# Joint first-layer tiles and a second split of four products in an attention and mixture-of-experts kernel

## The chip, the cores and the metric

The kernel is one program on one core of one Trainium2 chip. The metric is the device time of one execution in microseconds (us), from inputs in HBM to the output in HBM. Engines: PE (TensorE, matrix products), DVE (VectorE), ACT (ScalarE), POOL (GpSimd) and SP (SyncE, which here only issues DMAs). PEld is the loading of PE's weights.

## The reference

Attention in chunks of 32 queries with a little context and 8 memory keys gives `x` of 3072 tokens by 512 features. Then a mixture of 8 experts is computed densely: the routing weights `P` come from softmax logits by 8 rounds of row and column scaling, and every token goes through every expert.

```python
for e in range(E):                       # E = 8
    h = np.maximum(x @ w1[e], 0.0)       # 512 -> F = 1024
    ye = h @ w2[e]                       # 1024 -> 512
    out += P[:, e:e + 1] * ye
```

## The kernel before, in words

**Number form.** Every fp32 operand is held as two fp16 tiles, a high and a low part. One fp32 product is then three fp16 products (`PASSES`).

**Seven products.** From expert 1 on both layers are computed in a two-by-two block split with seven products P1 to P7 in place of eight. Its outputs are sums: in the first layer `c11` comes from P1 and P2; `c12`, `c22` and `c21` add P6, P7, P5, P3 and P4 in PSUM and in DVE or POOL adds. A block of weights or of tokens that a product needs is a sum of blocks made ahead (`wblock`, `xblock`).

**Units.** A unit n = 0..47 is one expert e = n // 6 on 512 tokens (u runs 0 to 5, and back for odd experts). It has two parts of work: the first layer of unit n, and the second layer (output) of unit n-1. The first layer goes over four feature groups `fp` of 256 features, two groups of 128 in each of the split's halves; here fp 0 and 1 are the front pair, fp 2 and 3 the second pair. The output of a unit is made by two generators (`output`, TH = 2), with seven products each of 12 matmuls of 128x256 in PSUM tiles yx, yy, yz. That is 168 matmuls for the output of a unit, and 168 for its first layer when no product is split again.

**A second split.** For units 15 to 47 (in unit 47 only pair 0), `inner(specs, op)` (L2389) splits three of the seven first-layer products (`op` 1, 5, 3, i.e. P2, P5, P3) by the same scheme once more: seven steps of matmuls with 128 columns. One call works for two entries at a time, the second pair of unit n and the front pair of unit n+1, so a step is six matmuls (L2447) into PSUM tiles ix, iy, iz; ACT reads them (L2498), and DVE adds (L2509, L2482), into fp32 buffers `m`, `m5`, `m3`. Where three products of both pairs are split, a unit has 126 matmuls of 128 columns in place of 72 of 256.

**First layer of one group.** `hidden` (L2552) runs the products of one fp into px, py, pz (matmuls in `product`, L2371), tiles of 128x256. Behind its matmuls each fp has: ACT reads (L2582, L2665, L2765), DVE adds (L2697, L2601, L2641), POOL adds for `c11` (L2675) and `c12` (L2717), then on the finished sums `c`: DVE sums `ss` (L2788, four of 128x256, or fewer and wider), ACT high part (L2800, 128x768) and DVE low part (L2838), ACT high part of the sums (L2830, 128x1024) and DVE low part of the sums (L2857, 128x1024). What they give, `h`, is the weight operand of the output matmuls.

**Output of a unit.** Each generator has ACT reads of its PSUM with the routing weight (L2976) and DVE adds into `acc` (L3018); POOL issues the DMAs that store `acc` (L3133), and SP issues the loads.

**Order.** A planner records tasks with a cost, a due time and dependencies. On PE each task depends on the one before (`last_pe`), so PE's order is that in which the generators are stepped; `WOVEN` (L3512) writes it out per unit, one letter per step: F, G (front pair), B, C (second pair), x, y (output), i, j, k (second split of P2, P5, P3). DVE, ACT, POOL and SP are put in order by due times, worked out from when PE uses what they make. So on those engines a row runs when it stands first in its queue and its inputs are there.

**Buffers.** Rings of tiles in SBUF: a taker waits for the last users of the tile before. Blocks of tokens come in by SP's DMAs in 256 KB pieces (`blocks`, L3463), in a ring of 10 and 11 slots.

## Time and profile before

| what | us |
|---|---|
| time, median of 3 runs | 1882.04 (1881.41 to 1883.43) |
| span of the profiled execution, first to last instruction | 1878.8 |
| PE busy in it | 1865.7 |
| DVE busy | 1511.8 |
| ACT busy | 1123.9 |
| POOL busy | 811.2 |

The span is what the engines' records cover; the time holds what lies around it as well. An engine's busy time is a sum over its instructions. A PE matmul's duration in the timeline includes the time that it drains; the rate of a run of matmuls is read from the starts of one group and the next.

### The profile page before, as it was taken

The page shows a single profiled execution, that of the slowest core. Times are in us where ns is not written, and L with a number is a line of the kernel's source. Part 1 is how long each engine was busy: PE and PEld are TensorE (multiplying, and loading weights), DVE is VectorE, ACT ScalarE, POOL GpSimd, SP SyncE. Part 2 cuts the span into 40 slices and gives each one's busy share as a digit, 9 for nine tenths or more (in the row PEclk, how much of TensorE's full clock was granted, in tenths as well). Part 3 has the DMA queues.
Part 4 walks back from the last instruction along what each step waited for, and adds up shares of the span by engine and source line. Part 5 has one row for each costly group of instructions (what it writes and reads, how often), then busy time and mean ns, then how long its engine had stood idle before and what let it go on. Part 6 is the DMA issues. An engine that isn't in the chain of part 4 may idle for free.

```text
span 1878.8 us, 52243 instructions
## 1 busy us (share of the span) xinstructions
PE 1865.7 (99%) x21167; PEld 1619.8 (86%) x21167; DVE 1511.8 (80%) x2664; ACT 1123.9 (60%) x2272; POOL 811.2 (43%) x994
## 2 busy tenths in 40 slices
PE   8999999999999999999999999999999999999999
PEld 5776676788888999999998999999999999999998
DVE  5886779788899778887889788897889778896564
ACT  6665454666676556656656665665666565565453
POOL 3631222525565345434556345643555335651231
PEclk9999999999999999999999999999999999999999
DMA  9968843297799767797677957887677976885553
GB/s 217 228 146 204 213 140 135 80 286 207 198 268 295 198 167 206 219 265 179 186 222 224 262 149 192 245 262 180 178 221 223 255 190 175 223 249 148 121 125 90
DMA packets 347293, 374.31 MB, mean 199 GB/s; under 512 B 123500, under 2 KB 261484, under 8 KB 345452
## 3 DMA queue, kind: packets, MB, share of 16 engines
q1 hardware_dynamic: 323436, 327.98, 57.1%
q0 software_dynamic: 23616, 43.00, 15.4%
q8 instruction: 166, 2.72, 0.6%
q14 instruction: 75, 0.61, 0.1%
HBM read 242.96 MB, written 133.18 MB: 200 GB/s over the span
## 4 chain that ended last, share of the span: by engine, by line
PE 96%; DVE 1%; DMA 1%; issue 1%; ACT 1%; POOL 0%; SPq 0%; POOLq 0%
PE px L2371 25%; PE yx L2371 23%; PE yz L2371 12%; PE ix_1c L2447 7%; PE yy L2371 6%; PE yp L3267 5%; PE pz L2371 4%; PE iz_1c L2447 3%; PE py L2371 2%; PE iy_1c L2447 2%; PE yp L3330 1%; PE pp L3184 1%; PE xp L1793 1%; PE sp L1715 1%; PE ta L1782 1%
## 5 line engine op out<-in xcount | busy, mean ns | idle before, releaser
L2371 PEld LDWEIGHTS <-h 128*128 128x128 f16 x6972 | 667.6, 98 | 72.9 <-DVE h L2857 0.9
L2371 PEld LDWEIGHTS <-w_all 128*128 128x128 f16 x5640 | 542.1, 98 | 64.2 <-issue 1.8
L2371 PE MATMUL yx<-w_all,h 128*128 128x256 f16 x3840 | 482.9, 273 | 0.6 <-DVE h L2857 0.6
L2371 PE MATMUL px<-x_whole,w_all 128*128 128x256 f16 x2976 | 363.0, 273 | 0.6 <-DMA x_whole<-xkeep 0.4
L3133 POOL DMA_DIRECT2D akeep<-acc x164 | 145.2, 908 | 258.9 <-DVE acc L3018 239.2
L2371 PE MATMUL yz<-w_all,h 128*128 128x256 f16 x1920 | 230.9, 273 | 0.0
L2857 DVE TENSOR_TENSOR h<-ss,h 128x1024 f16<-128x1024 f32 x158 | 198.4, 1257 | 13.5 <-ACT h L2830 13.2
L2830 ACT CAST h<-ss 128x1024 f16<-128x1024 f32 x166 | 172.6, 1040 | 51.8 <-DVE ss L2788 51.5
L2838 DVE SCALAR_TENSOR_TENSOR h<-c,h 128x768 f16<-128x768 f32 x166 | 179.2, 1084 | 9.7 <-ACT h L2800 9.7
L2788 DVE SCALAR_TENSOR_TENSOR ss<-c,ss 128x256 f32<-128x256 f32 x336 | 173.0, 515 | 3.8
L2447 PEld LDWEIGHTS <-wi 128*128 128x128 f16 x2340 | 157.0, 98 | 6.4
L2371 PE MATMUL px<-x,w_all 128*128 128x256 f16 x1248 | 152.9, 273 | 0.0
L2800 ACT ACTIVATE h<-c 128x768 f16<-128x768 f32 x166 | 137.6, 838 | 25.1 <-DVE c L2601 15.6
L962 POOL TENSOR_TENSOR w2f<-w2f 128x256 f32<-128x256 f32 x96 | 103.3, 1076 | 113.7 <-DVE wp L773 100.9
L2788 DVE SCALAR_TENSOR_TENSOR ss<-c,h 128x256 f32<-128x256 f32 (+1 forms) x248 | 145.9, 590 | 6.4 <-ACT h L2776 3.0
L3083 ACT ACTIVATE acc<-yx,pscale 128x256 f32<-128x256 f32 x82 | 38.7, 472 | 159.1 <-PE yx L2371 158.8
L962 POOL TENSOR_TENSOR w1b<-w1b 128x256 f32<-128x256 f32 x96 | 88.0, 917 | 86.6 <-ACT m_1c L2498 49.7
L2447 PEld LDWEIGHTS <-w_all 128*128 128x128 f16 x1755 | 119.5, 98 | 6.3 <-issue 0.5
L2717 POOL TENSOR_TENSOR c<-h,x_whole 128x256 f32<-128x256 f32 x130 | 101.5, 802 | 37.9 <-ACT h L2582 32.4
L2371 PE MATMUL yy<-w_all,h 128*128 128x256 f16 x960 | 114.0, 273 | 0.0
L3267 PE MATMUL yp<-w_all,h 128*128 128x512 f16 x480 | 110.3, 379 | 0.0
L2976 ACT ACTIVATE acc<-yx,pscale 128x256 f32<-128x256 f32 x164 | 76.8, 473 | 39.3 <-PE yx L2371 39.2
(287 smaller groups left out, 3077.7 us busy)
## 6 DMA issues: line engine op xcount, KB each, us to landing
x_whole<-xkeep SPq DMA_DIRECT2D x186, 256.0 KB
akeep<-acc POOLq DMA_DIRECT2D x164, 256.0 KB, 5.5
wkeep<-wp SPq DMA_DIRECT2D x48, 512.0 KB
w_all<-wkeep SPq DMA_DIRECT2D x84, 256.0 KB
w_all<-wkeep SPq DMA_DIRECT2D x42, 512.0 KB
wkeep<-wp SPq DMA_DIRECT2D x48, 384.0 KB
w2f<-in_moe_w_dram SPq DMA_DIRECT2D x32, 512.0 KB
w1fm<-in_moe_w_dram SPq DMA_DIRECT2D x28, 512.0 KB
```

The source lines that it names most:

```text
L962: lambda d=d, p=p, q=q, op=op: nc.gpsimd.tensor_tensor(d(), p(), q(), op=op),
L2371: nc.tensor.matmul(dst.t, a, b, start=(not more and n == 0), stop=(n == end), skip_group_check=more,)
L2447: nc.tensor.matmul(dst.t[:, k], left(k, op[0], wl), right(k, op[1], xl), start=(not more and n == 0 and k == 0), stop=(n == 2), skip_group ...
L2717: lambda: nc.gpsimd.tensor_tensor(c.t[:, 1], rr(1), m35[1](), op=ALU.add),
L2788: lambda: nc.vector.scalar_tensor_tensor(dst(), src(), 0.0, other(), op0=ALU.max, op1=op),
L2800: lambda: nc.scalar.activation(h.t[:, 0, 0:3], c.t, AF.Relu),
L2830: lambda: nc.scalar.copy(h.t[:, 0, 3:7], ss.t),
L2838: lambda: nc.vector.scalar_tensor_tensor(h.t[:, 1, 0:3].rearrange("p a n -> p (a n)"), c.t.rearrange("p a n -> p (a n)"), 0.0, h.t[:, 0, 0 ...
L2857: lambda: spare.tensor_tensor(h.t[:, 1, 3:7], ss.t, h.t[:, 0, 3:7], op=ALU.subtract),
L2976: lambda: nc.scalar.activation(acc.t[:, cols], src.t, AF.Copy, scale=f),
L3133: lambda a=a, dst=dst: nc.gpsimd.dma_start(dst, a.t, accum_op=ALU.add),
L3267: nc.tensor.matmul(py.t, hf.t[:, hl, where[fh], o : o + P], room(fp, WIDE * wl + DM * fh, WIDE * wl + DM * (fh + 1)), start=(fp == 0 and i ...
```

## The change

**Joint tiles.** `paired` takes the place of `hidden` for experts 1 to 7; `hidden` stays for expert 0. It works on both fps of a pair at once: px holds 128x2x256, a step is 12 matmuls (L2607) into it, and each DVE add (L2647), ACT read (L2637) and DVE sum (L2740) is 128x512 wide instead of two or more of 128x256. High and low parts (L2761, L2779, L2770, L2797) stay one for each fp, and of the sums' low parts the first of each pair is on POOL. The sums `c` have a ring of two buffers, `s` has one.

**Second split.** It begins at unit 14 (`DEEP`) for both pairs of the same unit. Expert 2 splits P2, P5, P3, as before; experts 3 to 7 split P4 as well. One call `inner(e, u, pair)` runs the three or four products of a pair together: seven steps of 9 or 12 matmuls with 128 columns (L2511), ACT reads (L2545) and DVE adds (L2556) of 128x3x128 or 128x4x128. Its results are in one buffer `m` for each pair (pair 0 in `stage_high`, pair 1 in `x_whole`), and part 3 of it is `rest`, on which the first layer works until its sums `d` and `a` (L2740) are made.

**First layer in a split unit.** P1 gives c11 (DVE, into `c`), which P6 waits for; P6 gives c12, which P7 waits for; P7 gives c22 and, with four split, c21. One POOL add of 128x512 (`m35`) joins P3's and P5's parts. The small POOL adds of `c11` and `c12` and the ACT reads between are gone.

**Order and buffers.** In `WOVEN` all fourteen steps of the second split (i pair 0, j pair 1) stand at the head of a unit. Token blocks have two rings, six slots for products 0, 4, 5 and four for 1, 2, 3, 6; the split sums of the tokens (`load_xi`) and of the weights (`fetch_wi`) come as 256 KB loads; tiles of SBUF are assigned anew.

```diff
-    def inner(specs, op=1):
-
-        nm = "_".join(str(i) for i in specs[0]) + f"c{op}"
-        (wop, xop), wsums, xsums, results = {
-            1: (P2, wi, xi, inners),
-            3: (P3, wi3, xi3, thirds),
-            5: (P5, wi5, xi5, fifths),
-        }[op]
+    inners = {}
+    ASIDES = ((0, 0), (1, 0))
+
+    def inner(e, u, pair):
+
+        nm = f"{e}_{u}_{pair}i"
+        ops = split_of(e)
+        z = len(ops)
         parts = []
         made = []
         used = []
-        for e, u, pair in specs:
+    inners = {}
+    ASIDES = ((0, 0), (1, 0))
+
+    def inner(e, u, pair):
+
+        nm = f"{e}_{u}_{pair}i"
+        ops = split_of(e)
+        z = len(ops)
         parts = []
         made = []
         used = []
-        for e, u, pair in specs:
+        for op in ops:
+            wop, xop = {1: P2, 5: P5, 3: P3, 4: P4}[op]
             tiles = [wblock(e, 2 * pair + i, 1, wop) for i in range(2)]
-            win, xin = wsums[e, pair], xsums[u]
+            win, xin = wi[e, pair, op], xi[u, op]
             x, part, xmade = xblock(u, xop)
-            parts.append((tiles, win, part, xin))
+            parts.append((tiles, win[0], part, xin[0], (0, 1, 2, 3) if op in (1, 4) else (3, 0, 2, 1)))
...
-        if op == 5:
-            m = rings["m5"].take(
-                lambda _: stage.tile([P, 2, 2, 2, P], F32, tag="stage_2", name=f"m5_{nm}")
-            )
-        elif op == 3:
-            m = rings["m3"].take(
-                lambda _: spare(5, 7).bitcast(F32).rearrange("p (k f q n) -> p k f q n", k=2, f=2, q=2)
-            )
-        else:
-            m = rings["m"].take(
-                lambda k: spare(3, 5).bitcast(F32).rearrange("p (k f q n) -> p k f q n", k=2, f=2, q=2)
-                if k
-                else stage.tile([P, 2, 2, 2, P], F32, tag="stage_3", name=f"m_{nm}")
-            )
-        z = len(specs)
-        if op == 3:
-            m5, _, ready5 = fifths[specs[0][0], specs[0][1], 2 * specs[0][2]]
-
-        which_op = op
+        m = rings["m"].take(
+            lambda k: (spare(3, 7).bitcast(F32) if k else high).rearrange(
+                "p (o f q n) -> p o f q n", o=4, f=2, q=2
+            ),
+            pair,
+        )
...
-                lambda: nc.scalar.activation(at(*to), src.t[:, 0:z], AF.Copy, scale=DOWN),
+                0.6,
...
+        inners[e, u, pair] = (m, [m11, m12, m22, read(ix, (1, 0), t4, ix)])
...
-    def hidden(e, u, fp, hs, use_at, aside, place="h"):
+    def paired(e, u, which, hs, place="h"):
+
+        nm = f"{e}_{u}_{which}"
+        fps = 2 * which, 2 * which + 1
+        px = bank("main", [P, 2, GT], f"px_{nm}")
+        c = rings["cd"].take(
+            lambda k: shaped(joint["c"] if k else both_sums(), [P, 2, 3, GT])
...
+                for f in range(2):
+                    for n, (kt, (wl, xl)) in enumerate(
+                        (kt, p) for kt in range(2) for p in PASSES
+                    ):
+                        nc.tensor.matmul(
+                            dst.t[:, f],
...
+        if (e, u, which) in inners:
+            m, made = inners[e, u, which]
+            part = lambda i: lambda: m.t[:, i].rearrange("p f q n -> p f (q n)")
+            m35 = add(
+                "POOL",
+                1.5,
+                lambda: nc.gpsimd.tensor_tensor(part(2)(), part(2)(), part(1)(), op=ALU.add),
+                made,
+                now[0],
+                [m],
+            )
+            t1 = run(px, P1, False, [], px)
+            c11 = plus(px, at(2), part(0), [t1, *made], [c, m])
+            yield
+            t6 = run(px, P6, True, [c11])
+            c12 = plus(px, at(1), part(2), [t6, m35], [c, m])
+            yield
+            rest = part(3)
+            t7 = run(px, P7, True, [c12])
+            if len(split_of(e)) == 4:
+                c22 = plus(px, at(0), part(1), [t7, *made], [c, m], px)
+                c21 = plus(px, rest, rest, [t7, *made], [m], px)
+                yield
...
+        s = rings["sd"].take(lambda k: shaped(joint["ss"], [P, 2, 4, GT]))
...
+        d = rsum(0, 0, rest, ALU.subtract, [r, c22], [m])
+        a = rsum(2, 2, rest, ALU.add, [r, c11], [m])
+        b = rsum(1, 0, lambda: s.t[:, :, 2], ALU.subtract, [a, c22])
+        g = rsum(3, 1, lambda: s.t[:, :, 1], ALU.add, [b, c12])
+        yield
...
+            aside = (which, f) in ASIDES
+            slo = add(
+                "POOL" if aside else "DVE",
+                2.15 if aside else 1.24,
...
-        "fine": "FGZiiFGiFiiGyixiyFGxyxjxjyjyjxjxjyjkkxykxykxykBkCkBCBCB",
...
+        "thirds": "ijijijijijijijFxyFxytFxyFFxyFxyBxyBtxyBxyBBxyxy",
+        "deep": "ijijijijijijijFxyFxyFxyFFxyBxyBxyBxyBxyxy",
+        "end": "ijijijijijijijFxByFxByFxByFFWBBxyxyxyxyxyxy",
...
-        specs = [(*units[n + i], 1 - i) for i in range(2) if thirded(n + i)] if not end else []
-        deep = [inner(specs, op) for op in (1, 5, 3)] if specs else []
+        inside = [inner(e, u, p) for p in range(2)] if deep else [None] * 2
```

**PE at the head of unit 25 (expert 4, second unit), before.** px is the first layer, yx the output, ix and iz the second split; "..." leaves out the rest of each group of six or twelve, and the weight loads.

```order
L2371 MATMUL px_0_3_16303<-x_whole_10012,w_all 128x256
...
L2447 MATMUL ix_1_1c_16402<-x_whole_10012,w_all 128x128
...
L2447 MATMUL iz_1_1c_16410<-xi_1_1_14807,wi_1_15351 128x128
...
L2371 MATMUL px_1_0_16374<-x_whole_9735,w_all 128x256
...
L2371 MATMUL px_1_1_16382<-x_whole_9735,w_all 128x256
...
L2447 MATMUL ix_1_1c_16402<-xi_1_1_14807,wi_1_15351 128x128
...
L2371 MATMUL px_1_0_16374<-x_whole_9735,w_all 128x256
...
L2447 MATMUL iz_1_1c_16410<-x_whole_10012,wi_1_15351 128x128
...
L2447 MATMUL ix_1_1c_16402<-xi_1_1_14807,wi_1_15351 128x128
...
L2371 MATMUL px_1_1_16382<-x_whole_9735,w_all 128x256
...
L2371 MATMUL yx_0_1_16482<-w_all,h_0_0_15813 128x256
```

The same place now; the names ending in 0i and 1i are the second split of pair 0 and of pair 1.

```order
L2448 MATMUL yz_0_1_15276<-w_all,h_late 128x256
...
L2511 MATMUL ix_1_0i<-x_whole_9177,w_all 128x128
...
L2511 MATMUL ix_1_1i<-x_whole_9177,w_all 128x128
...
L2511 MATMUL iz_1_0i<-wx_late 128x128
...
L2511 MATMUL iz_1_1i<-wx_late,p_all 128x128
...
L2511 MATMUL ix_1_0i<-wx_late 128x128
...
L2511 MATMUL ix_1_1i<-wx_late,p_all 128x128
...
L2511 MATMUL ix_1_1i<-wx_late,w_all 128x128
...
L2607 MATMUL px_1_0_15610<-x_whole_9477,w_all 128x256
...
L2448 MATMUL yx_0_0_15626<-w_all,h_all 128x256
...
L2448 MATMUL yx_0_1_15637<-w_all,h_all 128x256
```

Steps of six matmuls stood among steps of the first layer and the output. Now fourteen steps of twelve stand in one piece, and the first layer comes behind them.

**DVE at the same place, before.** acc is the output's sum, h_0_0 and h_0_1 take the low parts of sums, ss are the sums, x_whole the buffer of the second split.

```order
L2857 TENSOR_TENSOR h_0_0_15813<-ss_0_0_16068,h_0_0_15813 128x1024
L2788 SCALAR_TENSOR_TENSOR ss_0_1_16260<-c_0_1_15910,h_0_1_15816 128x2x256
L773 SCALAR_TENSOR_TENSOR wp_4_3_4_16245<-w2f_3_15992,sw,wp_4_3_4_16245 128x4x256
L3018 SCALAR_TENSOR_TENSOR acc_3_15990<-yz_0_1_16120,pscale,acc_3_15990 128x256
L2509 SCALAR_TENSOR_TENSOR x_whole_10012<-ix_0_1c_16147,x_whole_10012 128x2x128
L2788 SCALAR_TENSOR_TENSOR ss_0_1_16260<-c_0_1_15910,ss_0_1_16260 128x256 x2
L2509 SCALAR_TENSOR_TENSOR x_whole_10012<-iy_0_1c_16294,x_whole_10012 128x2x128
```

Now. ss_all from c_all and x_whole, twice, are `d` and `a` of unit 24's second pair, which read `rest` in pair 1's buffer.

```order
L3071 SCALAR_TENSOR_TENSOR acc_2_15132<-yz_0_0_15257,pscale,acc_2_15132 128x256
L3071 SCALAR_TENSOR_TENSOR acc_3_15147<-yz_0_1_15276,pscale,acc_3_15147 128x256
L2797 TENSOR_TENSOR h_all<-ss_all,h_all 128x1024
L2740 SCALAR_TENSOR_TENSOR ss_all<-c_all,x_whole_9477 128x2x256 x2
L2779 SCALAR_TENSOR_TENSOR h_all<-cs_late,h_all 128x768
L2779 SCALAR_TENSOR_TENSOR h_all<-c_all,h_all 128x768 x2
L2556 SCALAR_TENSOR_TENSOR stage_high<-iz_1_0i,stage_high 128x4x128
L2556 SCALAR_TENSOR_TENSOR stage_high<-ix_1_0i,stage_high 128x4x128
```

ACT in the same stretch, now; the row into x_whole is the first read of pair 1's second split in unit 25.

```order
L2770 CAST h_all<-ss_all 128x1024
L3139 ACTIVATE acc_0_15289<-yx_0_0_15082,pscale 128x256
L2770 CAST h_all<-ss_all 128x1024
L3139 ACTIVATE acc_1_15305<-yx_0_1_15093,pscale 128x256
L2761 ACTIVATE h_all<-c_all 128x768 x2
L2545 ACTIVATE stage_high<-ix_1_0i 128x4x128
L2545 ACTIVATE stage_high<-iz_1_0i 128x4x128
L2545 ACTIVATE x_whole_9477<-ix_1_1i 128x4x128
L2545 ACTIVATE x_whole_9477<-iz_1_1i 128x4x128
```

On DVE the low part of the sums stands between the last acc and the two sums that read pair 1's buffer, and ACT's first read into that buffer can run when both are made. Before, the reads of the second split go to buffers that take turns.

**DVE in unit 12 (first of expert 2), now.** c_all from py is the first layer's c11 of pair 1; h_late from ss_all is the low part of sums that the output of unit 11 uses.

```order
L3071 SCALAR_TENSOR_TENSOR acc_2_8635<-yy_0_0_8637,pscale,acc_2_8635 128x256
L3071 SCALAR_TENSOR_TENSOR acc_3_8655<-yy_0_1_8657,pscale,acc_3_8655 128x256
L2647 SCALAR_TENSOR_TENSOR c_all<-py_0_1_8710,c_all 128x2x256
L2797 TENSOR_TENSOR h_late<-ss_all,h_late 128x1024
L2182 TENSOR_TENSOR wx_late<-x_0_7565 128x512
L849 SCALAR_TENSOR_TENSOR wp_2_3_3_8731<-stage_high,sw,wp_2_3_3_8731 128x2x256
L886 TENSOR_REDUCE mxs<-w1fm_1_8701 128x1
```

Before, at the same place, c from px are adds of 128x256 of unit 12, and h_0_2 and h_0_3 the low parts for unit 11's output.

```order
L2601 SCALAR_TENSOR_TENSOR c_0_0_8950<-px_0_0_8899,q_2_0_0_8990 128x256
L2601 SCALAR_TENSOR_TENSOR c_0_1_8960<-px_0_1_8909,q_2_0_1_8993 128x256
L2857 TENSOR_TENSOR h_0_2_8786<-ss_0_2_8917,h_0_2_8786 128x1024
L2601 SCALAR_TENSOR_TENSOR c_0_0_8950<-pz_0_0_8964,h_0_0_8926 128x256
L2601 SCALAR_TENSOR_TENSOR c_0_1_8960<-pz_0_1_8972,h_0_1_8937 128x256
L2857 TENSOR_TENSOR h_0_3_8796<-ss_0_3_8979,h_0_3_8796 128x1024
```

The low part stood between two pairs of adds; now it stands behind one add of both groups, whose input is the PSUM tile py.

## Rows read from the trace of the kernel before

**Rows 1.** The page: the span, and busy time of each engine with its instructions.
```profile
span 1878.8 us, 52243 instructions
PE 1865.7 (99%) x21167; PEld 1619.8 (86%) x21167; DVE 1511.8 (80%) x2664; ACT 1123.9 (60%) x2272; POOL 811.2 (43%) x994
```

**Rows 2.** The page: shares of the chain that ended last, by engine.
```profile
PE 96%; DVE 1%; DMA 1%; issue 1%; ACT 1%; POOL 0%; SPq 0%; POOLq 0%
```

**Rows 3.** What PE waited for from 600 us on: total us, times, longest.
```profile
PE yx L2371 <- DVE h L2857: 0.6, 1, 0.6
PE px L2371 <- DMA x_whole<-xkeep: 0.4, 1, 0.4
PE px L2371 <- DVE c L2697: 0.2, 1, 0.2
```

**Rows 4.** PE's timeline near 1001 us: start, duration, instruction, count.
```profile
1000.84 0.50 PE L2447 MATMUL iz_1c<-x_whole,wi 128*128 128x128 f16 x6
1001.17 0.50 PE L2447 MATMUL ix_1c<-xi,wi 128*128 128x128 f16 x6
1001.51 0.82 PE L2371 MATMUL px<-x_apart,w_all 128*128 128x256 f16 x6
```

**Rows 5.** PE's timeline, 692 to 695 us.
```profile
692.13 1.47 PE L2371 MATMUL yz<-w_all,h 128*128 128x256 f16 x12
693.44 0.50 PE L2447 MATMUL ix_1c<-more,w_all 128*128 128x128 f16 x6
693.78 0.50 PE L2447 MATMUL ix_1c<-x_whole,w_all 128*128 128x128 f16 x6
694.11 0.33 PE L2447 MATMUL iz_1c<-xi,wi 128*128 128x128 f16 x3
694.28 0.33 PE L2447 MATMUL iz_1c<-more,wi 128*128 128x128 f16 x3
694.45 2.79 PE L2371 MATMUL yx<-w_all,h 128*128 128x256 f16 x24
```

**Rows 6.** The page: weight loads of the inner products, mean ns behind busy us.
```profile
L2447 PEld LDWEIGHTS <-wi 128*128 128x128 f16 x2340 | 157.0, 98 | 6.4
```

**Rows 7.** ACT's timeline, same stretch; idle time and its releaser in brackets.
```profile
692.00 0.47 ACT L2976 ACTIVATE acc<-yz,pscale 128x256 f32<-128x256 f32 x1
692.37 0.89 ACT L764 ACTIVATE ws_halves<-w1b,sw 128x256 f16<-128x256 f32 x2
693.64 0.47 ACT L2976 ACTIVATE acc<-yz,pscale 128x256 f32<-128x256 f32 x1 [0.38 <-PE yz L2371]
```

**Rows 8.** DVE's timeline, 691 to 697 us.
```profile
691.31 1.22 DVE L2857 TENSOR_TENSOR h<-ss,h 128x1024 f16<-128x1024 f32 x1
692.44 0.42 DVE L2509 SCALAR_TENSOR_TENSOR m_1c<-iy_1c,m_1c 128x256 f32<-128x256 f32 x1
696.36 0.68 DVE L2788 SCALAR_TENSOR_TENSOR ss<-c,h 128x512 f32<-128x512 f32 x1
```

**Rows 9.** DVE instructions by line and shape: busy us, mean ns, idle before.
```profile
L2857 DVE TENSOR_TENSOR h<-ss,h 128x1024 f16<-128x1024 f32 x158 | 198.4, 1257 | 13.5 <-ACT h L2830 13.2
L2788 DVE SCALAR_TENSOR_TENSOR ss<-c,h 128x512 f32<-128x512 f32 x84 | 64.1, 763 | 3.4 <-ACT h L2776 3.0
L3018 DVE SCALAR_TENSOR_TENSOR acc<-yz,pscale,acc 128x256 f32<-128x256 f32 x82 | 39.1, 478 | 17.2 <-PE yz L2371 17.0
L773 DVE SCALAR_TENSOR_TENSOR wp<-w2f,sw,wp 128x1024 f16<-128x1024 f32 x24 | 31.3, 1304 | 2.1 <-ACT wp L764 2.1
```

**Rows 10.** ACT instructions by line and shape.
```profile
L2830 ACT CAST h<-ss 128x1024 f16<-128x1024 f32 x166 | 172.6, 1040 | 51.8 <-DVE ss L2788 51.5
L2800 ACT ACTIVATE h<-c 128x768 f16<-128x768 f32 x166 | 137.6, 838 | 25.1 <-DVE c L2601 15.6 <-DVE c L2697 9.6
L1802 ACT COPY at<-ta 128x512 f32<-128x512 f32 x24 | 14.1, 587 | 7.8 <-PE ta L1782 7.7
```

**Rows 11.** What DVE waited for from 600 us on, by line.
```profile
DVE c L2697 <- PE px L2371: 54.9, 85, 1.5
```

More of the change, by code (lines that the diff above doesn't have):

```diff
@@ L56 @@
 LONG = 0.6
+BRIEF = 0.75
 LENGTHY = 0.4
@@ L61 @@
 PACED = 1
+EARLIER = 20.0
 BESIDES = 0.8
 class Task:
-    __slots__ = ("eng", "cost", "fn", "prio", "left", "ready", "end", "then", "takes", "frees", "n", "dma", "start", "size", "port", "also", "first", "lead")
+    __slots__ = ("eng", "cost", "fn", "prio", "left", "ready", "end", "then", "takes", "frees", "n", "dma", "start", "size", "port", "also", "first", "lead", "tag")
     def engines(self):
@@ L598, in sums_buf @@
     def sums_buf(kind, shape, name):
[L600 to L604 removed]
+        return rings[kind].take(lambda k: shaped(home(kind, k), shape))
     def bank(group, shape, name):
@@ L2361, in tile_chunked_attn_sinkhorn_moe, with product @@
     last_pe = [None]
-    def product(dst, pairs, more, deps, bufs=(), takes=None, parts=1, part=0):
+    def product(dst, pairs, more, deps, bufs=(), takes=None, parts=1, part=0, tag=None):
         def go():
@@ L2691, in hidden @@
[L2691 to L2705 removed]
+        py = psum("py")
@@ L2706, in hidden @@
+        q1, r1 = read(px, "q1", t1)
+        yield
+        t2 = run(py, P2, False, [], py)
+        c11 = plus(2, py, q1, [t2, r1])
+        yield
+        t6 = run(px, P6, True, [r1])
+        q6, r6 = read(px, "q6", t6)
+        yield
+        t5 = run(pz, P5, False, [], pz)
+        q5, r5 = read(pz, "q5", t5)
+        yield
+        t7 = run(px, P7, True, [r6])
+        c22 = plus(0, px, q5, [t7, r5], last=False)
         yield
-        if m is None:
-            t3 = run(pz, P3, True, [r5])
-            c12 = plus(1, pz, q6, [t3, r6])
-            yield
+        t3 = run(pz, P3, True, [r5])
@@ L2802, in hidden @@
+            lambda: nc.scalar.activation(h.t[:, 0, 0:4], c.t, AF.Relu),
+            [c11, c22, c12, c21],
             at - 6.0,
@@ L2952, in run @@
                 part,
+                "plain" if a < 3 else "sums",
             )
@@ L3111, in output @@
+        if DEEP - 1 <= n < len(units) - 1:
+            c21 = fourth()
+            yield
+            c12 = third()
+        else:
+            c12 = third()
+            yield
+            c21 = fourth()
         ended.setdefault(e, []).extend([c11, c12, c22, c21])
@@ L3552, in weave @@
         run(*front)
-        if end:
-            free = [t for g in range(6) for t in rings["wb"].last[1, 0, g].users]
-            for g in range(6):
-                rings["wb"].last[1, 0, g].closed = True
-            for i in range(2):
-                rings["w1"].after(i, free)
-            rings["w1"].n = 0
-            run(*pair(1, "w1"))
-        run(*deep[0:2])
-        run(*deep[2:3])
         run(*back)
         hidden_of.pop(n - 1)
-        behind[:] = then
-        if kind == "opening" or n == FINE * NU + 3:
-            run(*behind)
+        run(*then)
         if first_of:
@@ new lines, in weave @@
+            rings["xid"].after(2, wide)
+            fetch_wi(e, 0, begin(n))
+        if (n + 1) % NU:
+            blocks(n + 1)
+            load_xi(e, units[n + 1][1], begin(n), range(len(split_of(e))))
+        elif n + 1 < len(units):
+            if e == FINE:
+                for kind, k in (("xid", 3), ("wid", (0, 3))):
+                    rings[kind].after(k, rings["xt"].last[0].users)
+                rings["wid"].after((1, 3), [t for k in range(2) for t in rings["xg"].last[k].users])
+                load_xi(e, units[n + 1][1], begin(n), (3,))
+            for side in range(2):
+                fetch_w(e + 1, 1, side)
+                fetch_wi(e + 1, side, begin(n))
@@ L3772, in tile_chunked_attn_sinkhorn_moe @@
             expert_scale(e + 1, begin(n + 1))
+    ring("ss", range(2))
+    for i in range(2):
+        rings["ss"].after(i, rings["sd"].last[0].users)
+    rings["sd"].last[0].closed = True
     outputs(len(units) - 1, hidden_of.pop(len(units) - 1))
```

1082 lines of the change are left out of this document (513 added, 569 removed), and 12 rows, old and new, of the table TOKENS.

## The prediction, made before the run

> **What bounds the kernel now.** I read the page's busy times first: PE is busy 1865.7 of a span of 1878.8 us, the other engines 80% or less [rows 1]. Then the chain that ended last: 96% of it is PE, no other engine has more than 1% [rows 2]. Then PE's own waits from 600 us on, where every unit with a second split lies: three, 1.2 us in all [rows 3]. So PE's order runs almost without a gap, and its length is what the change can move, in two ways: the matmuls that PE has to run, and new places where PE finds its operand not made. DVE, ACT and POOL count only at such places.
>
> **The matmuls.** Twelve matmuls of 128x128 take from 1000.84 to 1001.51, 0.67 us or 55.8 ns each [rows 4]. Twelve of 128x256 start at 692.13 and the next group at 693.44: 1.31 us, 109.2 ns each [rows 5]. A split product has 126 or 168 narrow matmuls in a unit where it had 72 or 96 wide ones (three or four products). Before, 32.5 units of three: 4095 narrow in place of 2340 wide. Now four units of three and thirty of four: 4 x 126 + 30 x 168 = 5544 in place of 4 x 72 + 30 x 96 = 3168. The change therefore removes 828 wide and adds 1449 narrow: -828 x 0.1092 + 1449 x 0.0558 = -90.4 + 80.9 = **-9.5 us**. The output's matmuls, expert 0, expert 1's counts and the attention stay. The saving holds while the narrow ones keep their pace in runs of 168. The longest run that the trace has is 18, from 693.44 to 694.45, 56.1 ns each [rows 5]; at that figure the sum is -9.1.
>
> The Trainium skill, "TensorE: Matmul & The Clock Gate", section "Back-to-back issue gap", speaks against this: a sustained stream of weight load and matmul costs about 81 ns at 128 columns there, not 56. By its figure the sum would be 1449 x 0.081 - 90.4 = +27 us, an estimate. The run of 18 does not bear it out; runs of 168 are not in this trace.
>
> **DVE, ACT, POOL, DMA.** Most of their edits I cost at nothing, since PE's work hides them: the joint adds and sums need half as many instructions of twice the width (a sum of 128x512 takes 0.68 undisturbed [rows 8] and 0.76 in the mean, an add of 128x256 0.48 [rows 9]), so no engine gets more to do and DVE stays below PE. POOL, busy 43% [rows 1], loses small adds and gets `m35` and half the sums' low parts. If a queue's order is wrong this cover is gone; that is the next part. SP's loads grow by about 256 KB a unit, with wider windows of time between buffer free and use; I take 0, with 0 to +1.
>
> **New waits.** I looked for places where the rows that stand on an engine between a matmul group and the matmul that needs their result last longer than PE's work between. PE's results reach another engine 0.20 us after the next group has started: yz's next group starts at 693.44, ACT's read of yz at 693.64 [rows 5, 7]. In a full queue a DVE row starts about 0.08 before the end of the one ahead (691.31 + 1.22 against 692.44) [rows 8], an ACT row about 0.10 (692.00 + 0.47 against 692.37) [rows 7]. I take 0.04 for a semaphore between engines (yz ends at 692.13 + 1.47 = 693.60, ACT starts 693.64).
>
> Unit 12: the sums' low part stands behind the add of c11, which needs py. 0.20 + 0.60 (128x512, 0.68 less 0.08) + 1.22 + 0.04 = 2.06 us [rows 8] after py's last matmul; in PE's order its reader comes 5 matmuls, 0.55 us, after. **1.5 us.** Queued behind the waiting row are preparations of the next expert's weights, which are not due soon.
>
> Unit 14, the first with a split at its head: in ACT's queue two high parts and one high part of sums stand between an inner read and the next. 0.20 + 0.38 + 2 x 0.74 + 0.94 + 0.48 + 0.04 = 3.5, where 0.74 and 0.94 are 0.84 and 1.04 less 0.10, and 0.48 stands for a read of 128x384, somewhat less than 0.59 for 128x512 [rows 10] (0.38 with its overlap). That is against four steps of nine matmuls, 2.0: **1.4 us** (a weight load that waits for the same pair's sums lies inside it).
>
> Units 19, 25, 31, 37, 43, each the second of an expert: pair 1's buffer is read by the sums d and a of the unit before, and these stand behind the last acc and a low part of sums. From the last output matmul: 0.20 + 0.40 (acc) + 1.14 (low part) + 0.60 (d) + 0.68 (a) + 0.04 + 0.59 (ACT's read of 128x512 [rows 10]) = 3.65, or 3.8 where a semaphore takes away two overlaps of 0.08. PE comes to it after five steps of twelve narrow matmuls, 3.35. That is 0.3 to 0.5, I take **0.45 us in each of four**. In unit 19 a weight preparation of 128x1024 stands there too, 1.30 less 0.08 [rows 9]: **1.5 us**.
>
> Named waits: 1.5 + 1.4 + 1.5 + 4 x 0.45 = **6.2 us**. Durations are here those of undisturbed rows; the means are longer (low part 1.26, 128x512 0.76 [rows 9]), so 6.2 is nearer the lower end: 5 to 10.
>
> **The rest.** The 1.2 us of late waits belong to code that is replaced, -1.2. Places that are tight without being late by the count: P1 gives c11 gives P6 inside 12 matmuls of output, 1.31 against 0.20 + 0.68 + 0.04 = 0.92; with c12 and c22, and two pairs, six such links a unit. What the spread of durations cost before is those 1.2 us; with wider rows I take 2.2, from 0 to +8.
>
> **Sum.** -9.5 + 6.2 - 1.2 + 2.2 = -2.3 us on the span of 1878.8: 1876.5. Around the span lie 1882.0 - 1878.8 = 3.2 us. So **1879.7 us**, its own range 1877 to 1883.5. What a measurement of this kernel can tell from no change is about 0.2%, 3.8 us: 1878.3 to 1885.8.
>
> **Rivals.**
>
> B, the saving shows. PE's wait at one place gives the other engines the time that they lack at the next, and in a unit's first 9.4 us (168 narrow matmuls) they have only inner reads and adds to serve, so queues may run ahead of the order's count. If only units 12 and 14 are late, 2.9 us, and nothing else: -9.5 - 1.2 + 2.9 = -7.8, **1874.2 us**. For it: three waits in 1280 us before. Against: in units 19 to 43 the first row of the path is itself released by the last output matmul, so no head start helps.
>
> C, slower: the link P1, c11, P6. Its margin is 0.39 us. If a low part (1.26) or another wide row has just begun on DVE when px is ready, c11 starts late and PE stands still for what exceeds 0.39, in every split unit. At 0.35 us a unit, 34 units: +11.9, **1891.6 us**. It decides from the point where DVE reaches c11's row more than 0.39 us after px. For it: rows are twice as wide and the links go through DVE with no other product of the pair between. Against: the narrower link to P4 before (L2697) had DVE idle in front of it 85 times, 54.9 us of waiting for px [rows 11], and PE waited there once, 0.2 us [rows 3].
>
> D, the long run falls out of pace. A weight load of the narrow kind has a mean of 98 ns [rows 6], longer than the 55.8 between starts, and can hide only beside matmuls that are under way; behind wide ones it has time, in a run of 168 narrow ones it may not. If each of the 1449 added ones had to wait for its whole load, that is 42 ns more: +61 us, **1941 us**. Against: in the run of 18 the last starts are as close as the first [rows 5]. By the Trainium skill's figure above it would be 1879.7 + 36 = 1916, an estimate.
>
> That the change doesn't do what it says is excluded for the counts: PE's order has them.
>
> **Chances.** Forecast 0.50, of which 0.13 lies below 1878.3 and 0.37 within the bound; B 0.26, nearly all faster; C 0.20, of which 0.17 is beyond 1885.8 and 0.03 within; D 0.04. Together faster 0.38, same 0.41, slower 0.21. The range 1873 to 1888 takes in B and the near part of C and leaves out a fifth: below it only B with hardly any wait (-12 would be 1870), above it C in full and D.
>
> **What would show it.** Right: 5544 narrow matmuls at 55.8 ns; 168 in 9.4 us; PE's waits in the changed kernel naming DVE's low part in unit 12, ACT's inner read in units 14, 19, 25, 31, 37, 43, with 6 us together; PE's busy time about 9 us down. Wrong: PE waits on L2607 for c11 in many units (C); a narrow group of twelve taking over 0.7 us inside the long run (D); an added DMA wait at xf, xn or xi blocks, which I priced at nothing; or no wait at units 25 to 43 (B).

## The result, and the profile after

The changed kernel takes 1906.4 us (median of 4 runs, 1903.4 to 1909.3) against 1882.0; the ratio is 1.0126 with an interval of 1.011 to 1.0142. It is slower by 24 us, and outside the range of 1873 to 1888 that was predicted. The profiled execution is the slowest of the four (1909.3, span 1907.5).

From the page of the changed kernel: the span, the busy times and the chain by engine, to be set beside [rows 1, 2].

```profile
span 1907.5 us, 52507 instructions
...
PE 1865.1 (98%) x21788; PEld 1624.9 (85%) x21788; DVE 1525.2 (80%) x2203; ACT 1063.0 (56%) x1804; POOL 914.5 (48%) x950
...
PE 88%; DVE 3%; DMA 3%; ACT 2%; issue 2%; SPq 0%; POOL 0%; DVEq 0%; POOLq 0%; ACTq 0%
```

PE's busy time is about what it was, though it has 1449 more narrow and 828 fewer wide matmuls; it also counts the stretches at a slower clock, which come below. Its share of the chain fell from 96% to 88%. DVE, DMA, ACT and issue took that share. Next, what PE waited for in the whole execution, longest sums first; the rows of the attention part are left out. [Rows 3] had 1.2 us from 600 us on.

```profile
PE px L2607 <- DVE cs_late L2647: 10.6, 6, 2.4
PE iz_1i L2511 <- DMA p_all<-wikeep: 5.0, 1, 5.0
PE px L2607 <- ACT cs_late L2637: 4.4, 1, 4.4
PE ix_1i L2511 <- ACT x_whole L2545: 3.3, 5, 1.4
PE px L2607 <- DVE c_all L2647: 2.0, 2, 1.1
...
PE yx L2448 <- DVE h_late L2797: 1.4, 1, 1.4
PE ix_1i L2511 <- DMA w_all<-wkeep: 1.4, 1, 1.4
```

To see where each wait lies I took the starts of all matmuls of this execution and subtracted from the distance between two starts what one takes undisturbed (109.2 ns at 256 columns, 55.8 at 128, as in [rows 4, 5]). "A slower clock" in the table is a stretch behind a wait in which PE's granted clock was 0.50 to 0.60 of full speed. What is left over, from 300 us on:

| place | us lost | what PE waited for |
|---|---|---|
| units 22, 28, 34, 40 (959, 1178, 1396, 1613 us) | 4 x 2.57, and 3.2 at a slower clock behind two of them | DVE's c12, behind a weight preparation that took 5.0 us |
| unit 9's scaling (462 us) | 7.2, of it 2.6 at a slower clock | ACT's read, behind a scaling whose load was late |
| unit 14 (652 us) | 6.6, of it 1.5 at a slower clock | the load of pair 1's weight sums |
| unit 12 and unit 19 (591, 839 us) | 1.6 and 1.6 | the low part; ACT's first read into pair 1's buffer |
| units 25, 31, 37, 43 | 4 x 0.61 | the same read |
| units 26 and 32 (1112, 1330 us) | 1.0 and 1.3 | DVE's c11, behind rows that waited for a load |
| unit 18 (799 us) | 1.6 | a load of weight blocks |
| other places | 2.1 | |

Together 38.9 us; the kernel before lost 3.1 in the same count, 35.8 less. The matmuls undisturbed take 9.6 us less. The first 300 us lost 2.7 more, which no run here explains. 35.8 + 2.7 - 9.6 = +28.9, and the spans differ by 28.7: the account closes. It is that of the slowest execution; the medians differ by 24.

**Unit 28, where the largest kind lies.** PE's timeline: the output group of 12 ends, and P7 waits 2.41 us for c12 (`cs_late`).

```profile
1174.46 1.47 PE L2448 MATMUL yx<-w_all,h_all 128*128 128x256 f16 x12
1178.34 1.47 PE L2607 MATMUL px<-x_whole,w_all 128*128 128x256 f16 x12 [2.41 <-DVE cs_late L2647]
```

DVE's timeline there: a weight preparation (L849) that takes 4.99 us, then c12.

```profile
1172.70 4.99 DVE L849 SCALAR_TENSOR_TENSOR wp<-w1b,sw,wp 128x512 f16<-128x512 f32 x1
1177.61 0.68 DVE L2647 SCALAR_TENSOR_TENSOR cs_late<-px,stage_high 128x512 f32<-128x512 f32 x1
```

POOL's timeline in the same stretch: four rows that follow each other without a gap, the last until 1174.73 + 2.40 = 1177.13.

```profile
1172.68 0.75 POOL L1370 TENSOR_TENSOR ws_halves<-w1b,w1b 128x128 f32<-128x128 f32 x1
1173.09 1.55 POOL L2662 TENSOR_TENSOR stage_high<-stage_high 128x512 f32<-128x512 f32 x1
1174.32 0.74 POOL L1370 TENSOR_TENSOR ws_halves<-w1b,ws_halves 128x128 f32<-128x128 f32 x1
1174.73 2.40 POOL L2797 TENSOR_TENSOR h_all<-ss_all,h_all 128x1024 f16<-128x1024 f32 x1
```

The preparation is one row of 128x512 with two inputs in SBUF. A row of the same kind at unit 12 took 0.74:

```profile
591.23 0.74 DVE L849 SCALAR_TENSOR_TENSOR wp<-stage_high,sw,wp 128x512 f16<-128x512 f32 x1
```

The one at unit 28 started with the first POOL row of the string and ended 0.56 after the last. At units 22, 34 and 40 the same row takes 4.98 to 4.99 beside the same four POOL rows. So it looks as if it was held until the string was over; e1 tests that. The Trainium skill, "SBUF — State Buffer", section "🔬 SBUF: two separate sides", says that GpSimd and a DVE operation with two SBUF inputs share a pair of ports under an exclusive lock: the one that starts first has it for its whole instruction, and the other is blocked. The rows agree with that for the first POOL row, 0.02 us ahead of DVE's; what they add is that DVE did not get in between the four rows either. Which engine came first is not settled by starts so close: in e1 below DVE's start is recorded 0.11 us ahead of POOL's, and DVE was held all the same.

**Unit 25, a wait that was predicted.** PE's timeline (12 matmuls in 0.67 us, as predicted, and the wait), then DVE's and ACT's.

```profile
1052.79 0.83 PE L2511 MATMUL ix_0i<-x_whole,w_all 128*128 128x128 f16 x12
1053.46 0.83 PE L2511 MATMUL ix_1i<-x_whole,w_all 128*128 128x128 f16 x12
...
1056.76 0.49 PE L2511 MATMUL ix_1i<-wx_late,p_all 128*128 128x128 f16 x6 [0.45 <-ACT x_whole L2545]
```

```profile
1052.99 0.48 DVE L3071 SCALAR_TENSOR_TENSOR acc<-yz,pscale,acc 128x256 f32<-128x256 f32 x1 [0.82 <-PE yz L2448]
1053.39 1.22 DVE L2797 TENSOR_TENSOR h_all<-ss_all,h_all 128x1024 f16<-128x1024 f32 x1
1054.72 1.29 DVE L2740 SCALAR_TENSOR_TENSOR ss_all<-c_all,x_whole 128x512 f32<-128x512 f32 x2
```

```profile
1056.11 0.60 ACT L2545 ACTIVATE x_whole<-ix_1i 128x512 f32<-128x512 f32 x1 [0.51 <-DVE ss_all L2740]
```

The acc of the last output, the low part, and then `d` and `a` (L2740, two rows); ACT's read into pair 1's buffer waits 0.51 for them.

**Unit 14.** SP issued the load of pair 1's weight sums at 644.87, after a wait for the sums of unit 13; PE had it at 651.93, 7.1 us later. SP's wait and timeline, then PE's:

```profile
SPq L1250 <- DVE ss_all L2740: 2.9, 1, 2.9
...
644.87 0.34 SPq L1250 DMA_DIRECT2D p_all<-wikeep  x1
```

```profile
651.93 0.80 PE L2511 MATMUL iz_1i<-wx_late,p_all 128*128 128x128 f16 x6 [5.00 <-DMA p_all<-wikeep]
```

**Near 462 us.** ACT's timeline: the scaling (L2940) waits for its load, the row behind it is a high part, and the third is the read (L2637) that PE waits for.

```profile
460.15 0.51 ACT L2940 ACTIVATE p_all<-p_all,pscale 128x256 f32<-128x256 f32 x1 [5.93 <-DMA p_all<-akeep]
460.56 0.83 ACT L2761 ACTIVATE h_late<-c_all 128x768 f16<-128x768 f32 x1
461.30 0.58 ACT L2637 ACTIVATE cs_late<-px 128x512 f32<-128x512 f32 x1
```

**Units 26 and 32, a load on DVE's queue.** At unit 26 DVE waited 1.52 us for a load before it could reduce it (L757). Seven rows follow it almost without a gap before c11, so c11 came late, and PE waited for it:

```profile
1108.49 0.42 DVE L757 TENSOR_REDUCE most_of<-ws_halves 128x2 f32<-128x256 f32 x1 [1.52 <-DMA ws_halves<-mkeep_wNone]
...
1111.74 0.68 DVE L2647 SCALAR_TENSOR_TENSOR c_all<-px,x_whole 128x512 f32<-128x512 f32 x1
```

```profile
1112.47 1.25 PE L2607 MATMUL px<-x_whole,w_all 128*128 128x256 f16 x10 [0.84 <-DVE c_all L2647]
```

At unit 32 the wait for a load of the same kind is 1.80 us. No run moved these rows, so this reading rests on the rows alone.

### The profile page after: what moved, and what is told of

It is laid out like the page before. It is cut to its first block, busy times and chain, and to the rows that moved or that the text cites. A ratio compares the mean times of both kernels' runs of the same rounds, so it can differ in the third digit from the quotient of the medians.

```text
span 1907.5 us, 52507 instructions
## 1 busy us (share of the span) xinstructions
PE 1865.1 (98%) x21788; PEld 1624.9 (85%) x21788; DVE 1525.2 (80%) x2203; ACT 1063.0 (56%) x1804; POOL 914.5 (48%) x950
## 4 chain that ended last, share of the span: by engine, by line
PE 88%; DVE 3%; DMA 3%; ACT 2%; issue 2%; SPq 0%; POOL 0%; DVEq 0%; POOLq 0%; ACTq 0%
PE yx L2448 21%; PE px L2607 18%; PE yz L2448 11%; PE yy L2448 6%; PE yp L3333 5%; PE ix_1i L2511 4%; PE ix_0i L2511 4%; PE px L2448 2%; PE iz_1i L2511 2%; PE iz_0i L2511 2%; PE pz L2607 2%; PE pz L2448 1%; PE iy_1i L2511 1%; PE iy_0i L2511 1%; PE yp L3396 1%
## 5 line engine op out<-in xcount | busy, mean ns | idle before, releaser
L2448 PEld LDWEIGHTS <-h_all 128*128 128x128 f16 x4704 | 461.8, 98 | 55.3 <-DVE h_all L2779 0.2
L2607 PEld LDWEIGHTS <-w_all 128*128 128x128 f16 x3888 | 380.1, 98 | 63.4 <-issue 18.6
L2448 PE MATMUL yx<-w_all,h_all 128*128 128x256 f16 x2592 | 325.6, 273 | 0.0
L2607 PE MATMUL px<-x_whole,w_all 128*128 128x256 f16 x2544 | 313.6, 273 | 11.9 <-DVE cs_late L2647 9.9
L2448 PEld LDWEIGHTS <-h_late 128*128 128x128 f16 x2268 | 221.8, 98 | 27.4 <-DVE h_late L2797 1.7
L2797 POOL TENSOR_TENSOR h_all<-ss_all,h_all 128x1024 f16<-128x1024 f32 x56 | 126.1, 2251 | 145.8 <-ACT h_all L2770 126.9
L2448 PE MATMUL yx<-w_all,h_late 128*128 128x256 f16 x1248 | 163.7, 273 | 1.4 <-DVE h_late L2797 1.4
L2448 PE MATMUL yz<-w_all,h_all 128*128 128x256 f16 x1296 | 165.0, 273 | 0.0
L2647 DVE SCALAR_TENSOR_TENSOR cs_late<-px,stage_high 128x512 f32<-128x512 f32 x102 | 70.4, 690 | 87.7 <-PE px L2607 69.4
L2511 PEld LDWEIGHTS <-w_all 128*128 128x128 f16 x2376 | 136.9, 98 | 2.4 <-DMA w_all<-wkeep 1.6
L2770 ACT CAST h_all<-ss_all 128x1024 f16<-128x1024 f32 x112 | 114.1, 1039 | 27.5 <-DVE ss_all L2740 27.5
L2545 ACT ACTIVATE stage_high<-ix_0i 128x512 f32<-128x512 f32 (+1 forms) x102 | 59.6, 585 | 101.3 <-PE ix_0i L2511 99.9
L2797 POOL TENSOR_TENSOR h_late<-ss_all,h_late 128x1024 f16<-128x1024 f32 x27 | 59.7, 2211 | 91.6 <-ACT h_late L2770 86.5
L2607 PE MATMUL px<-x,w_all 128*128 128x256 f16 x768 | 95.4, 275 | 5.2 <-ACT cs_late L2637 4.4
L3333 PE MATMUL yp<-w_all,h_all 128*128 128x512 f16 x432 | 100.0, 379 | 0.0
L2647 DVE SCALAR_TENSOR_TENSOR c_all<-px,x_whole 128x512 f32<-128x512 f32 x102 | 70.1, 687 | 31.9 <-PE px L2607 31.0
```

The costliest lines, as they stand in the source:

```text
L2448: nc.tensor.matmul(dst.t, a, b, start=(not more and n == 0), stop=(n == end), skip_group_check=more,)
L2511: nc.tensor.matmul(dst.t[:, k], left(k, op[0], wl), right(k, op[1], xl), start=(not more and n == 0 and k == 0), stop=(n == 2), skip_group ...
L2545: lambda: nc.scalar.activation(at(*to), src.t, AF.Copy, scale=DOWN),
L2607: nc.tensor.matmul(dst.t[:, f], ws[f][1](wl, kt), part(xl, kt), start=(not more and f == 0 and n == 0), stop=(n == 5), skip_group_check=True,)
L2647: lambda: nc.vector.scalar_tensor_tensor(to(), src.t, DOWN, other(), op0=ALU.mult, op1=ALU.add),
L2770: lambda f=f, h=h: nc.scalar.copy(h.t[:, 0, 3:7], s.t[:, f]),
```

## The experiments

Each was run beside the kernel before on the same chip; its median there was 1882.0 to 1882.6 in every comparison.

### POOL waits for the DVE row (e1)

```diff
-            t.fn()
+            made = t.fn()
...
+                    if slotted[2] is not None and made is not None and before_[0] - LOCK - 0.02 <= slotted[0] and at - before_[0] < 1.5:
+                        tc.add_manual_dep(made.ins, slotted[2].ins.name, mybir.DependencyInfo(mybir.DependencyClass.Sync, mybir.DependencyReason.DATA), reason="yield")
...
```

The added line is for a row `t` on POOL that the planner had put right behind a DVE row of two SBUF inputs (`slotted`): it now waits for that row. Every engine's rows stand in the order of the changed kernel.

> Changed kernel with its order kept; some 210 POOL rows get one more wait: a POOL row that the planner had put behind a DVE row of two SBUF inputs now waits for that DVE row. Theory 1 (a DVE row with two SBUF inputs gets nothing done while POOL rows follow each other without a gap): the DVE rows of 5.0 us at units 22, 28, 34 and 40 (a weight preparation of 128x512 that takes 0.7 alone) fall below 2.7, the four PE waits of 2.57 us behind them fall below 0.8, the held rows near 1112 and 1330 us likewise; time 8 to 14 us less, about 1895. Rival (c12 is late there because of the order of DVE's queue or a late input): the waits stay at 2.5 and the time stays within 3 us of 1906 or grows by the added waits.

Measured: 1891.4 us (1889.1 to 1893.0), 15.0 less than the changed kernel. At unit 28, DVE's rows, then POOL's, then PE's:

```profile
1166.70 2.63 DVE L858 SCALAR_TENSOR_TENSOR wp<-w1b,sw,wp 128x512 f16<-128x512 f32 x1
1169.26 0.68 DVE L2656 SCALAR_TENSOR_TENSOR cs_late<-px,stage_high 128x512 f32<-128x512 f32 x1
```

```profile
1166.81 0.76 POOL L1379 TENSOR_TENSOR ws_halves<-w1b,w1b 128x128 f32<-128x128 f32 x1
1167.22 1.55 POOL L2671 TENSOR_TENSOR stage_high<-stage_high 128x512 f32<-128x512 f32 x1
1169.48 0.46 POOL L1379 TENSOR_TENSOR ws_halves<-w1b,ws_halves 128x128 f32<-128x128 f32 x1 [0.70 <-DVE wp L858]
```

```profile
1168.45 1.47 PE L2457 MATMUL yx<-w_all,h_all 128*128 128x256 f16 x12
1169.99 1.47 PE L2616 MATMUL px<-x_whole,w_all 128*128 128x256 f16 x12
```

The same DVE row takes 2.63, since only one short and one long POOL row stand ahead of the added wait; it ends 0.56 after the long one, and the next POOL row waits 0.70 for it. PE loses 0.23 in place of 2.57 (1169.99 - 1168.45 against 1.31). At units 22, 34 and 40 no wait over 0.12 is left. With the order the same, only the string was changed: theory 1, that POOL's strings hold the DVE row in front of c12, holds here, and is shown. One part of the expectation was missed: of the waits near 1112 and 1330 us the second went, but that of unit 26 grew from 1.0 to 1.9. DVE waited there 2.59 us for the load of `ws_halves`, and no POOL string is needed for that.

### All low parts on DVE (e2)

```diff
-    ASIDES = ((0, 0), (1, 0))
+    ASIDES = ()
```

> All low parts of sums on DVE, none on POOL (64 rows of 2.2 us leave POOL, as many of 1.2 us come to DVE). Theory 1: the POOL strings are shorter by their longest rows, the 5.0 us DVE rows come down to about 3 or less, the four waits of 2.57 to under 1; but DVE gets some 80 us more to do and its order changes, so new waits of some us; time 1890 to 1905. Rival (order of DVE's queue): with DVE fuller the waits grow, time over 1910.

Measured: 1891.6 us (1889.8 to 1898.8), 14.8 less. PE's longest waits from 300 us on:

```profile
PE ix_1i L2511 <- ACT x_whole L2545: 4.7, 4, 1.2
PE iz_1i L2511 <- DMA p_all<-wikeep: 3.6, 1, 3.6
...
PE px L2607 <- DVE cs_late L2647: 0.7, 2, 0.5
```

The planner's order moved as well, and 84 low parts left POOL, not the 64 of the expectation. The wait for c12 is 0.7 in all, from 10.6. No DVE row is longer than its kind's usual time by 3 us; the changed kernel had six. The losses at the heads of units 25, 31, 37 and 43 grew to 1.34 each. At unit 25 that is not the buffer: DVE's `d` and `a` end at 1043.28, and ACT's read into it, at 1044.41, stands behind a read of pair 0 that waits 0.74 for PE. The change raised the low parts of sums on POOL, rows of 2.2 us, from 8 to 84, and in the order made for them they cost more there than on DVE in the order of e2.

### Unit 14's second split in two pieces (e3)

```diff
+        "first": "iiiiiiiFxyFxytFxyjjjjjjjFFxyFxyBxyBtxyBxyBBxyxy",
...
```

> Only unit 14 differs: its second split of pair 0 stands first, that of pair 1 after three steps of the first layer. Theory (pair 1's weight sums can be loaded only when the sums of unit 13 have read the buffer, and such a load needs some 5 us from its issue to its landing): the wait of 5.0 us at 652 us, 6.6 with the slower clock behind it, falls below 1, time 5 to 7 us less, about 1900. Rival (loads of that stretch are slow because the DMA queues are full, wherever PE asks): the wait moves to pair 1's first step and stays over 2 us, time within 3 us of 1906.

Measured: 1902.7 us (1898.8 to 1905.8), 3.7 less; the intervals of the ratios overlap, so the place says more than the time. PE's longest waits from 300 us on:

```profile
PE px L2607 <- DVE cs_late L2647: 8.5, 6, 2.4
PE px L2607 <- ACT cs_late L2637: 4.5, 1, 4.5
```

The load's wait of 5.0 is gone from the list; unit 14 loses 1.65 in small pieces in place of 6.6. The rival's wait at pair 1's first step, over 2 us, did not come. So the wait was a matter of how soon PE asked; how much of it is the buffer that came free late (SP waited 2.9 for it) and how much the 7.1 us of the load, e3 doesn't separate. The other waits are not quite as they were, since the planner moved rows: that of unit 22 is gone, those of units 28, 34 and 40 stand.

### Three products in all split units (e4)

```diff
-        return OPS[:3] if e == FINE else OPS
+        return OPS[:3]
...
```

> Experts 3 to 7 split three products as expert 2 does, so 30 units have 96 wide and 126 narrow first-layer matmuls in place of 72 and 168. By the count PE has 30 x (24 x 0.1092 - 42 x 0.0558) = 8.3 us more. If the waits come from POOL strings, DMA landings and the head-of-unit buffer they stay about the same: time 1906 + 8 = 1914. If the fourth split product itself causes them (c21 and a wider m on DVE and ACT): the waits of units 22, 28, 34, 40 shrink, time 1895 to 1905.

Measured: 1897.9 us (1897.2 to 1898.4), 8.5 less, though PE's undisturbed sum is 8.3 more. PE's longest waits:

```profile
PE px L2607 <- ACT cs_late L2637: 5.5, 1, 5.5
PE iz_1i L2511 <- DMA p_all<-wikeep: 4.0, 1, 4.0
PE px L2607 <- DVE c_all L2647: 3.8, 3, 1.6
...
PE px L2607 <- DVE cs_late L2647: 1.3, 2, 0.7
```

The rival, that the fourth product itself costs more than its matmuls save, came true in the time: the waits for c12 shrank to 1.3 in all, and those at the heads are gone; the waits for c11 grew from 2.0 to 3.8. That does not make the fourth product their cause by itself (e1 and e2 remove them with four), but in the order that the planner made for four, strings stand where c12 is waited for. In e4's order no DVE row of these units is longer than 2.7 us. The two late loads stand as before.

### Pair 0 two steps ahead (e5), the low part ahead of c11 (e6)

```diff
-        "deep": "ijijijijijijijFxyFxyFxyFFxyBxyBxyBxyBxyxy",
...
+        "deep": "iijijijijijijjFxyFxyFxyFFxyBxyBxyBxyBxyxy",
...
```

> Only the order of the second split in units 18 to 47 differs: two steps of pair 0 ahead of pair 1's first, which comes 0.67 us later. Theory (PE waits there for pair 1's buffer, which the sums d and a of the unit before release 0.6 us late, 1.6 in unit 19): the four waits of 0.61 us at units 25, 31, 37, 43 go to 0.1 or less and that of unit 19 falls from 1.61 to about 0.95; 3 us less in all, unless the planner moves other rows. Rival (ACT's queue is late there whatever the buffer): the waits stay.

One run, 1894.9. The head waits are 0.31 at 1268, 0.22 at 1697 and below 0.12 elsewhere, that of unit 19 is gone. That alone would also fit a late queue on ACT, since PE comes 0.67 us later; that it was the buffer is in the rows of unit 25 above, where ACT's read waits for `d` and `a`. Most of the 11 us that the run is shorter has another cause: the planner moved rows, and at units 28 and 34 c12 was late by 0.3 and less (at unit 22 still by 2.7).

```diff
+            low = [h[2][1] for h in hidden_of.get(e * NU + u - 1, [])[1::2]] if (e, u, which) == (FINE, 0, 1) else []
-            c11 = plus(py, at(2), at(2), [t2, r1], [c], py)
+            c11 = plus(py, at(2), at(2), [t2, r1, *low], [c], py)
```

`low` holds unit 11's low parts, in unit 12 alone.

> Only unit 12 differs: the add of c11 of pair 1 is put behind the low parts of unit 11's sums. Theory (the low part stood behind a row that waits for PE): the wait of 1.61 us at 590 us falls below 0.3 and none as large comes near it; time 1 to 1.6 us less, within the spread of the runs. Rival (the low part is late for its own input): the wait stays above 1 us.

One run, 1907.1. The wait of 1.61 at unit 12 is gone and none is in its place; the time is within the spread of the changed kernel, and says nothing.

### Together, and the scaling near 462 us (e7 to e10)

e7 has the edits of e1, e3, e5 and e6.

> POOL's added waits, unit 14's order, pair 0 two steps ahead, and unit 12's low part, together. If the four causes are apart and add up: 1891.4 (POOL's waits alone) - 6.0 (unit 14) - 3.0 (heads) - 1.5 (unit 12) = about 1881, the waits from 300 us on 11 to 13 us in place of 38. If the planner's new order brings other held rows or late loads, 1885 to 1892.

Measured: 1884.9 us (1881.3 to 1888.3), ratio to before 1.0015 (1.0005 to 1.0025). It lost 15.5 us from 300 us on, 7.0 of them near 464 us. PE's longest wait:

```profile
PE px L2616 <- ACT cs_late L2646: 4.9, 1, 4.9
```

The time is 3.9 above the 1881 of four causes that add up, at the lower edge of the other case (1885 to 1892); the losses from 300 us on, 15.5, are also somewhat more than the 11 to 13 expected. Two tries at the last large wait made the planner count a later landing, for all scalings (e8) or for unit 9's (e9):

```diff
-                    late = GUARDS.get(s.eng, 0.0)
+                    late = GUARDS.get(s.eng, 0.0) + (3.5 if id(s) in self.slow else 0.0)
...
```

> As the one before, and the planner counts 3.5 us more for the loads whose scaling on ACT stood in front of the first layer's reads near 460 us. If that wait (7.2 us in the changed kernel) is ACT's queue standing behind a load that lands late: it falls below 2, time 4 to 6 us below the kernel before in this list, about 1876. If the reads are late for another reason the wait stays over 4 us and the time is the same as without.

> As e7, and the planner counts 3.5 us more for the landing of the loads that unit 9's scaling on ACT waits for (for this unit alone), so that two first-layer reads stand ahead of the scaling near 460 us and not behind it. If the wait of 5 to 7 us there (5.0 and its slower clock in e7) is ACT's queue standing behind a late load: it falls below 1.5 us and the time is about 1885 - 6 = 1879, 2 to 4 us below the kernel before. Rival (the reads are late for their own input, or the load holds something else that PE needs): the wait stays above 3 us, time 1883 to 1886.

Both missed: 1890.6 (1886.6 to 1896.5) and 1887.6 (1886.0 to 1893.3). The wait near 462 us went in both (in e9 1.5 and 3.0 came at 462 to 468 for a low part), but the planner's whole order behind it moved, and new losses of 1.8 to 5.3 us came at 432, near 580 and at 886 us in e8, and of 2.0 and 1.2 near 588 in e9. So in e10 the planner's order was kept: one row of ACT moves behind four others, and its store on SP with it, nothing else.

```diff
+            if T == 10 and i % 2 == 0:
+                plan.hold = s
...
```

> As e7 with one ACT row moved: the first scaling of unit 9 (and SP's store of it) stands four ACT rows later, behind the two first-layer reads that it stood ahead of; no other row changes its place. If PE's wait of 5.0 us at 464 us (7.0 with the slower clock) is those reads standing behind the scaling's late load: it falls below 1 us and the time is 1885 - 6 = 1879, about 3 us below the kernel before. Rival (the reads are late for something else): the wait stays above 3 us and the time at 1885.

Measured: **1880.6 us** (1876.6 to 1886.5, 12 runs), ratio to the kernel before 0.9983 (0.9973 to 0.9994). It beats the changed kernel by 26 us and the kernel before by 2 us in the median; the second interval is just clear of 1, and the difference is below the 3.8 us that the prediction took as the least that can be told from no change. Of the 6 us expected, 4 came in the median. The expected case came for the read that the scaling had held: PE's wait of 4.9 for px is gone. In the profiled execution, which is the slowest, PE now waits 2.7 there for the next read, of pz. That read stands behind another ACT row, a conversion of `wx_late` (L2227), which waits 4.79 us for POOL.

```profile
PE px L2628 <- DVE c_all L2668: 3.7, 2, 2.4
PE pz L2628 <- ACT cs_late L2658: 2.7, 1, 2.7
```

The 3.7 for c11 (`c_all`) are units 26 and 38. At both DVE had waited for the load of `ws_halves` in front of it, 2.22 and 3.21 us, as at unit 26 of the changed kernel. That cause none of the mended versions touches.

### The fourth product in the mended order (e11)

The edit of e4 on e10.

> The mended kernel of e10 with three products split in place of four in experts 3 to 7. By PE's count 30 x (24 x 0.1092 - 42 x 0.0558) = 8.3 us more than e10. If a mended order leaves the count to decide, the time is 1880.6 + 8.3 = 1889, between 1886 and 1891. If the fourth split brings waits of its own even in the mended order: 1880 to 1885, no slower than e10 by more than 3 us.

Measured: 1884.1 us (1881.6 to 1890.7), 3.5 more than e10 and not the 8.3 of the count, between the two cases. Set against the kernel before, each in its own comparison, the ratios are 1.0010 (1.0000 to 1.0019) and 0.9983, which makes about 5 us. Its profiled execution lost 7.9 us from 300 us on, e10's 16.7 (its slowest run). So the fourth split is worth some 3.5 to 5 us, and 3 to 5 of its 8.3 go into waits that three products don't have. Which of them, and whether the split or the planner's other order makes them, these runs leave open.

## Why the prediction was wrong, by its steps

- **The matmuls, -9.5 us: right.** 5544 narrow ones at 55.8 ns, wide ones at 109.2; undisturbed sum -9.6. The narrow pace held in the run of 168 (12 in 0.67 us at 1052.79 and at 1053.46), so rival D is not borne out. Nor does the figure hold here that the Trainium skill gives for a sustained stream at 128 columns, 81 ns ("TensorE: Matmul & The Clock Gate", "Back-to-back issue gap"). The sign "PE's busy time about 9 us down" did not come (1865.1 against 1865.7): 7.3 us at the slower clock count as busy.
- **The new waits, 6.2 us: right in six of the seven places, and 12.2 in all.** Unit 12: 1.5 predicted, 1.61 measured. Unit 19: 1.5 and 1.61. Units 25, 31, 37, 43: 0.45 and 0.61 each. Unit 14: 1.4 predicted for ACT's queue (its own terms, 3.52 less 2.01, give 1.5), 6.6 measured for a load. The step said that this load "lies inside it". It took 7.1 us from issue to PE. The step looked at the row that waits and not at the time of a landing, though the page before gives 5.5 us for the same size on POOL's queue.
- **"Most of their edits I cost at nothing, since PE's work hides them": this step failed.** It counted each engine's busy time, and POOL's was low. It did not ask which POOL rows stand back to back beside which DVE row. The joint add `m35` and the low parts put rows of 1.5 and 2.2 us on POOL, and strings of four rows with both in them held a DVE row for 5.0 us in front of c12. That is 13.5 us at units 22, 28, 34 and 40, clock included; e1 took back 15 us by breaking such strings, and e2 14.8 by taking the longest rows out of them. The trace before had such rows. The low part of [rows 9] has a mean of 1257 ns beside 1.22 undisturbed [rows 8], and the prediction met that with "Durations are here those of undisturbed rows" where it was a matter of neighbours. A clearer sign was not shown: near 512 us a preparation of 128x256 took 3.71 us, where 0.48 is usual, beside two POOL rows, the second a low part of 2.44.
- **"SP's loads ... I take 0": this failed too.** Late loads at unit 14, at unit 9's scaling and at unit 18 cost 15.4 us in the profiled execution, and with units 26 and 32, where the load held DVE's queue, 17.7. For the first two e3 and e10 show it; the others are read from the rows. These are not the added loads of token blocks that the term had in mind, but loads that come late.
- **Rival C** had the direction, and P7's link c12 is one of its kind, but not the mechanism: c11 and c12 are in time in most split units, and late by 2.57 in four (a held row) and by about 1 in two (a row that waited for a load).
- **The unlisted waits, 2.2 us**, were meant for small overruns; those came to 2.1 us. **Slower clock behind a long wait** had no term at all: 7.3 us, which are counted above in the places where they stand.
- **The sum, as measured:** -9.6 (matmuls) + 12.2 (the seven places) + 13.5 (POOL's strings) + 11.1 (the other late loads) + 2.1 - 3.1 (the kernel before) + 2.7 (the first 300 us) = 28.9 us.
